# Attention scores of whole jobs: from half-row float32 pairs to two whole-array float32r passes a head

## The chip, the cores and the metric

The kernel runs on one core of one Trainium2 chip. The metric is device time in microseconds of one execution. Three runs of the kernel before were timed; the comparison is between medians.

## The reference, cut to what matters

```
scores = scale * q @ k.T                     # 4 batches, 8 heads, 576 tokens, head size 64
cum    = cumsum(max(s, 0))
scores = where(causal, -1e9, scores + min(-(cum[q] - cum[k]), 0))
attn   = softmax(scores);  x = attn @ v      # x: 2304 tokens x 512
h = x @ w_in;  g = s * relu(h)**2 + b;  y = g @ w_out          # 512 -> 2048 -> 512
out = max(y@w1, y@w2, y@w3) @ w_out2                           # 512 -> 768 -> 512
```

The score of a query and a key is a product over 64 numbers plus a difference of two running sums, the decay. All arithmetic has to be close to float32.

## The kernel before, in words

Matrix products of the two MLPs are made of three float32r passes (`mm3`, lines 245 to 247): each operand is split into hi and lo, and hi·hi, hi·lo and lo·hi are summed in one PSUM bank. float32r is the type in which TensorE takes one pass over the columns.

Attention goes by jobs. A job is a pair of heads of one batch. The four pairs of the first batch are cut into half jobs, A (queries 0 to 319) and B (the rest), 8 in all; the other three batches are 12 whole jobs, W. Queries are cut into chunks of 64, 128, 128, 128 and 128, and the scores of a W job into 6 units of 64, 192, 320, 448, 288 and 288 key columns, 1600 in all (`UNITS`). For each unit `qk` issues four products: for each head a float32 product of q and k over 64 rows (line 468; head 0 on rows 0 to 63, head 1 on rows 64 to 127), and then for each head a float32r product over the same 64 rows (line 470), which adds the decay: `oh` picks the row of the head out of `dd`, the table of decay differences. VectorE adds the causal mask and takes the smallest (`least`, 482), ScalarE takes the exponential (`expo`, 488), TensorE turns the result (`turn_p`, 529), ScalarE or VectorE copies it to SBUF (`copy_p`, by `copy`, 234 or 238), and `av` (548) multiplies by v. The result x is split into hi and lo (GpSimd makes lo, `minus`, 241) for the first MLP.

Products of the first MLP fill TensorE between the steps of attention; the second MLP follows. Beside attention, VectorE, ScalarE and GpSimd also turn the MLP weights from float64 into hi and lo (`weight_steps`, 274 to 289). The first 16 pieces (`wa_in`, `wa_out`) are needed while the half jobs run, and W jobs use their staging memory, so the turned scores of the first W job wait for the last of them. Further pieces (`wb`, `wbs`) are converted beside the W jobs and saved to memory.

The order on every engine is fixed when the program is built. `Plan.order` is a list scheduler: each step has a cost, a due time and needs, and each engine's queue is written in the order that the plan finds. `PORT` and `has_port` make it keep GpSimd's steps and VectorE's conversion steps apart in its own reckoning. On the chip each engine works its queue in order and waits on semaphores. All loads and stores are issued by SP, in order. Score banks, turned scores, transposed reciprocals and their copies share a ring of four PSUM banks (`sm`).

Of the kernel before, what the change touches and what calls it, by code (L numbers as in the profile page):

```python
# [8 lines left out]
F32 = mybir.dt.float32  # L9
# [9 lines left out]
P = 128  # L19
# [13 lines left out]
K_LOAD = -14.0  # L33
V_LOAD = 2.0
# [158 lines left out]
def fused_kernel(ctx, tc, q, k, v, s, w_in, w_out, ms, mb, w1, w2, w3, w_fin, out,  # L193
# [224 lines left out]
    qt, kt, ohs, mns, ps_, pts, rts, rbs, pr, px_, xs_ = ({} for _ in range(11))  # L418
# [44 lines left out]
    def qk(job, u):  # L463
# [120 lines left out]
    def in_us(fixed, each):  # L584
# [8 lines left out]
                 "ws": 2, "wg": 3, "wx": 1, "wb": 3, "p": 3, "ph": 4, "wst": ST2, "wsa": 2, "xs": XS_BUFS, "y0": 2, "y": 2, "g2": 2, "yt": 2, "yh": 2, "u": 2, "o": 2})  # L593
# [30 lines left out]
    add(("pp",), "Pool", 1.2, 4.0, [("pre", "Pool")], rest_p, att=True)  # L624
    jobs = [Job(n, n % NP, "AB"[n // NP]) if n < 2 * NP else Job(n, n - NP, "W") for n in range((B + 1) * NP)]
    t0 = 0.0
    for job in jobs:
# [4 lines left out]
        for u, w in zip(units, widths):  # L632
            at[u] = t
            t += period * w / sum(widths)
# [8 lines left out]
        tp = t0 + TURN  # L643
        for key, when, m in (("q", Q_LOAD, job.q1 - job.q0), ("k", K_LOAD, job.keys)):
            add((key, n), "SP", (1, m), t0 + when, [("qk", n - 2, u) for u in range(6)], load_qk, job, key, **a)
        add(("v", n), "SP", (2, job.keys), t0 + V_LOAD, [("av", n - 2, g) for g in (jobs[n - 2].groups if n > 1 else ())], load_v, job, **a)
        add(("oh", n), "Pool", 0.3, tp, [("qk", n - 2, u) for u in range(6)], one_hot, job, **a)

        for x, u in enumerate(units):
            i, k0, k1, c0, c1 = UNITS[u]  # L650
            same = [("turn_p", n - 1, z, j) for z in range(6) if UNITS[z][0] == i for j in range(2)]
            order = [("after", ("qk", n, units[x - 1]))] if x else [("after", ("qk", n - 1, jobs[n - 1].units[-1]))] if n else []
            ready = [("oh", n), ("q", n), ("k", n)]
            add(("qk", n, u), "PE", 5 * (k1 - k0) / 2400 + 0.25, at[u], ready + [("dd", i) if i > 2 else ("pre", "DVE")] + [("after", z) for z in same] + order, qk, job, u,
                take=[("sm", [("least", n, u, j)]) for j in range(2)], **a)
# [14 lines left out]
        for x, u in enumerate(units):  # L670
            i, k0, k1, c0, c1 = UNITS[u]
            for j in range(2):
                t = at[u] + D_T + 0.2 * j
                before = (n, units[x], 0) if j else (n, units[x - 1], 1) if x else (n - 1, jobs[n - 1].units[-1], 1) if n else None
# [4 lines left out]
                if x == 0:  # L679
# [3 lines left out]
                    over += [("dd", NC - 1)]  # L683
# [426 lines left out]
```

## Time and profile before

| | |
|---|---|
| median of 3 runs | 947.61 us (947.55 to 948.44) |
| span of the profiled execution, first to last instruction | 945.5 us |
| the profiled execution's own time | not listed apart from its span; the median run is 2.1 us above the span |
| TensorE | 925.6 us busy, 98% |
| VectorE, ScalarE, GpSimd | 503.0, 422.2 and 162.2 us busy |

A span is counted from the first to the last instruction. A busy time is the union of the times in which an engine's instructions ran. TensorE's instructions overlap: a product is listed from its start to the modelled end of its drain, so what one costs is read from the distance between the starts of two.

### The profile page before, as it was taken

How to read it: one execution, taken by the hardware profiler on the slowest of the kernel's cores; microseconds unless marked ns; L12 is line 12 of the kernel's file. 1: busy time of each engine (PE TensorE's matmuls, PEld its weight loads, DVE VectorE, ACT ScalarE, POOL GpSimd, SP SyncE). 2: the span in 40 equal slices, each digit the busy share in tenths (PEclk: the TensorE clock that was granted, in tenths of full speed). 3: DMA queues.
4: the chain of work that ended last, by engine and by line, in shares of the span. 5: the costliest groups of instructions: out<-in, count | busy, mean ns of one | idle time of the engine just before them, and what ended most of it. 6: DMA issues, size and time to landing. Idle time of an engine off the chain costs nothing.

```text
span 945.5 us, 16334 instructions
## 1 busy us (share of the span) xinstructions
PE 925.6 (98%) x6016; PEld 848.6 (90%) x6016; DVE 503.0 (53%) x1322; ACT 422.2 (45%) x1126; POOL 162.2 (17%) x255
## 2 busy tenths in 40 slices
PE   7999899999999999999999999999999999999997
PEld 5677677778898799999999999999999999999997
DVE  6999788787833422224686687578621223121221
ACT  5987578888645643333353344344221212121111
POOL 3232122310412043222232133120000000000000
PEclk7999999999999999999999999999999999999999
DMA  7545464465522101912334324334120202010000
GB/s 231 172 122 163 155 197 152 135 192 163 159 80 71 35 16 54 371 55 84 102 121 152 118 85 134 117 117 134 51 68 1 67 1 67 1 51 1 23 12 34
DMA packets 68240, 96.00 MB, mean 102 GB/s; under 512 B 6592, under 2 KB 47296, under 8 KB 68160
## 3 DMA queue, kind: packets, MB, share of 16 engines
q1 hardware_dynamic: 68064, 94.81, 31.4%
q8 instruction: 47, 0.77, 0.3%
q14 instruction: 33, 0.27, 0.1%
q10 hardware_dynamic: 96, 0.15, 0.0%
HBM read 67.67 MB, written 27.26 MB: 100 GB/s over the span
## 4 chain that ended last, share of the span: by engine, by line
PE 90%; DMA 4%; ACT 2%; DVE 2%; SPq 1%; POOL 1%; issue 0%; DVEq 0%; ACTq 0%; POOLq 0%
PE mm L245 24%; PE mm L247 24%; PE mm L246 24%; PE ps L468 6%; PE pt L529 6%; PE px L548 5%; PE ps L470 1%; PE pr L519 1%; DMA xs<-x_d 1%; DMA wb_in<-wb_d 1%; DMA wg<-in_moe_w_in_dram 1%; DMA stage<-in_moe_w_out_dram 1%; ACT pp L488 0%; POOL ga L241 0%; DMA wbs<-in_moe_w_in_dram 0%
## 5 line engine op out<-in xcount | busy, mean ns | idle before, releaser
L245 PE MATMUL mm<-yh,wt 128*128 128x384 f32 x432 | 146.2, 339 | 0.0
L246 PE MATMUL mm<-yl,wt 128*128 128x384 f32 x432 | 146.2, 338 | 0.0
L247 PE MATMUL mm<-yh,wt 128*128 128x384 f32 x432 | 146.2, 338 | 0.0
L1017 DVE TENSOR_TENSOR u<-mm,u 128x384 f32<-128x384 f32 x72 | 40.1, 557 | 185.1 <-PE mm L247 184.9
L881 ACT ACTIVATE g<-g 128x384 f32<-128x384 f32 (+2 forms) x112 | 53.6, 479 | 155.2 <-DVE g L877 155.0
L488 ACT ACTIVATE pp<-pp,mn 64x64 f32<-64x64 f32 (+4 forms) x160 | 88.3, 556 | 12.8 <-DVE mn L482 12.8
L877 DVE TENSOR_SCALAR g<-mm 128x384 f32<-128x384 f32 (+2 forms) x112 | 55.5, 497 | 55.4 <-PE mm L247 49.0
L245 PE MATMUL mm<-ga,wa_out 128*128 128x320 f32 (+2 forms) x256 | 81.8, 320 | 1.5 <-ACT wa_out L234 1.5
L245 PEld LDWEIGHTS mm<-yh,wt 128*128 128x128 f32 x432 | 81.1, 188 | 1.3
L246 PEld LDWEIGHTS mm<-yl,wt 128*128 128x128 f32 x432 | 81.1, 188 | 1.3
L247 PEld LDWEIGHTS mm<-yh,wt 128*128 128x128 f32 x432 | 81.1, 188 | 0.0
L234 ACT ACTIVATE pt<-pt 128x256 f32<-128x256 f32 (+3 forms) x182 | 71.5, 434 | 20.7 <-PE pt L529 17.2
L245 PE MATMUL mm<-xhi,wa_in 128*128 128x320 f32 (+1 forms) x256 | 80.0, 312 | 0.0
L247 PE MATMUL mm<-ga,wa_out 128*128 128x320 f32 (+2 forms) x256 | 75.9, 297 | 3.5 <-DVE wa_out L289 3.5
L1021 ACT ACTIVATE hh<-u 128x384 fp32r<-128x384 f32 x36 | 18.9, 524 | 134.5 <-DVE u L1017 134.5
L529 PE MATMUL pt<-ident,pp 128*128 128x128 f32 x480 | 76.5, 283 | 2.3 <-ACT pt L234 1.0
L468 PE MATMUL ps<-k,q 64*128 64x288 f32 (+4 forms) x384 | 73.0, 449 | 3.8 <-DVE mn L482 3.5
L246 PE MATMUL mm<-ga,wa_out 128*128 128x320 f32 (+2 forms) x256 | 75.9, 297 | 0.5 <-POOL ga L241 0.5
L241 POOL TENSOR_TENSOR gbl<-g,gbh 128x384 fp32r<-128x384 f32 x48 | 51.1, 1064 | 145.0 <-ACT gbh L234 132.4
L247 PE MATMUL mm<-xhi,wa_in 128*128 128x320 f32 (+1 forms) x256 | 75.8, 296 | 0.0
L246 PE MATMUL mm<-xlo,wa_in 128*128 128x320 f32 (+1 forms) x256 | 75.7, 296 | 0.0
L482 DVE CUSTOM_DVE_ANT_0 pp<-late_keys,ps 64x64 f32<-64x64 f32 (+4 forms) x160 | 61.8, 421 | 21.0 <-PE ps L470 20.3
(158 smaller groups left out, 2143.2 us busy)
## 6 DMA issues: line engine op xcount, KB each, us to landing
wst<-in_moe_w_dram SPq DMA_DIRECT2D x24, 384.0 KB, 3.9
wb_d<-wbs SPq DMA_DIRECT2D x21, 256.0 KB, 2.6
k<-in_k_dram SPq DMA_DIRECT2D x16, 288.0 KB, 3.5
xs<-x_d SPq DMA_DIRECT2D x24, 192.0 KB, 3.0
y<-y_d SPq DMA_DIRECT2D x24, 192.0 KB, 3.3
y_d<-y SPq DMA_DIRECT2D x24, 192.0 KB, 2.5
yt<-y_d SPq DMA_DIRECT2D x24, 192.0 KB, 2.5
out_dram<-o SPq DMA_DIRECT2D x18, 256.0 KB, 2.0
```

What stands on the lines that cost most here:

```text
L234: nc.scalar.activation(dst, src, AF.Copy, scale=1.0 if scale is None else scale)
L241: ENGINES[on].tensor_tensor(dst, a, b, op=ALU.subtract)
L245: nc.tensor.matmul(ps, lhs[0], rhs[0], start=first, stop=False)
L246: nc.tensor.matmul(ps, lhs[0], rhs[1], start=False, stop=False)
L247: nc.tensor.matmul(ps, lhs[1], rhs[0], start=False, stop=last)
L468: nc.tensor.matmul(ps[:, :k1 - k0], qt[job.n][r, QS[i]:QS[i] + P], kt[job.n][r, k0:k1], start=True, stop=False)
L482: nc.vector.tensor_tensor_reduce(out=pp[j][i][:n, k0:k1], in0=late_keys[:n, a:a + k1 - k0], in1=ps_.pop((job.n, u, j))[:n, :k1 - k0], scal ...
L488: nc.scalar.activation(p[:n, :w], p[:n, :w], AF.Exp, bias=mns[job.n, j][:n, i:i + 1], scale=-1.0, accum_out=sums[job.n % 2][:n, j, i:i + 1])
L529: nc.tensor.transpose(pt[:, c - c0, :], pp[j][i][:, c * P:(c + 1) * P], ident)
L548: nc.tensor.matmul(px_[job.n][hf][j * D:(j + 1) * D, a0 - h0:h1 - h0], vn[job.n % 2][:, c, j, :], columns(job, pr["p", job.n, j], c, c + 1 ...
L877: nc.vector.tensor_scalar(st["g", f], st["u", f][:, :n], 0.0, None, op0=ALU.max)
L881: nc.scalar.activation(st["g", f], st["g", f], AF.Square)
```

## The change

A W job's scores are computed per head, by two float32r products over all 128 rows. A tile `set` holds four rows of tables for one head. QA is hi of q on rows 0 to 63 and lo of q on rows 64 to 127; KA is hi of k on both halves: their product is hi·hi plus lo·hi. KB has lo of k on rows 64 to 127, QB hi of q there: hi·lo. Rows 0 to 3 of KB and QB hold the running sum in hi and lo and ones, so that the decay comes out of the second product; the other rows of that half are zero, cleared once. So `oh` and the 64-row products remain for half jobs alone.

Making a set takes new steps for each of the 24 heads: a load of q and k, written twice so that both halves of the partitions hold them (`load_both`), one rounding on ScalarE over 128 x 1152 (`round_set`), one subtraction on GpSimd over 64 x 1152 (`rest_set`), one copy over 64 x 576 on GpSimd or ScalarE (`again_set`), and one small load of the decay rows (`decay_set`). Once, at the start, the running sums are split and saved to memory (`decays`, `save_d`) and the sets are cleared. Half jobs load each operand in two loads of 64 partitions in place of one of 128. Units of a W job go through head 0 and then head 1. The host lays q and k out accordingly, and the scratch memory for dynamic DMAs is set to 1024.

```diff
-    qt, kt, ohs, mns, ps_, pts, rts, rbs, pr, px_, xs_ = ({} for _ in range(11))
+    raw, hs_, ohs, mns, ps_, pts, rts, rbs, pr, px_, xs_ = ({} for _ in range(11))
+    QA, KA, KB, QB = range(4)
+    def decays(x, on=None):
+        c = cum[:NH]
+        if x == 0:
+            nc.scalar.activation(dm[:, 0], c, AF.Copy, scale=1.0 / scale)
+        elif x == 1:
+            nc.vector.scalar_tensor_tensor(dm[:, 1], c, 1.0 / scale, dmf[:, 0], op0=ALU.mult, op1=ALU.subtract)
...
+    def save_d():
+        for z in range(2):
+            nc.sync.dma_start(dm_d[:, z, 2 * z:2 * z + 2], dmf[:, 2 * z:2 * z + 2])
+            nc.sync.dma_start(dm_d[:, 1 - z, 2 * z:2 * z + 2], ones[:NH].unsqueeze(1).to_broadcast([NH, 2, S]))
...
     def load_qk(job, key):
 
-        to, src, a, b = (qt, q, job.q0, job.q1) if key == "q" else (kt, k, 0, job.keys)
-        to[job.n] = atp.tile([P, S], F32, name=key, tag=f"{key}{job.n % 2}")
-        nc.sync.dma_start(to[job.n][:, a:b], src[job.p, :, a:b])
+        z, src, a, b = (0, q, job.q0, job.q1) if key == "q" else (1, k, 0, job.keys)
+        if key == "q":
+            raw[job.n] = atp.tile([P, 2, S], F32, name="raw", tag=tag("raw"))
+        for j in range(2):
+            nc.sync.dma_start(raw[job.n][j * D:(j + 1) * D, z, a:b], src[job.p, j, :D, a:b])
+
+    def load_both(job, j):
+
+        t = raw[job.n, j] = atp.tile([P, 2, S], F32, name="raw", tag=tag("raw"))
+        for z, src in ((0, q), (1, k)):
+            nc.sync.dma_start(t[:, z], src[job.p, j])
+
+    def round_set(job, j):
+        hs_[job.n, j] = sets(plan.slot("hs")[1])
+        nc.scalar.activation(hs_[job.n, j][:, :2], raw[job.n, j], AF.Copy)
+
+    def again_set(job, j, on):
+        copy(hs_[job.n, j][D:, QB], raw[job.n, j][D:, 0], on)
+
+    def rest_set(job, j):
+        t = hs_[job.n, j]
+        minus(t[D:, QA:KB + 1:KB], raw[job.n, j][D:], t[D:, :2].bitcast(F32), "Pool")
+
+    def decay_set(job, j):
+        nc.sync.dma_start(hs_[job.n, j][0:4, KB:].bitcast(F32), dm_d[2 * job.p + j].rearrange("t r n -> r t n"))
...
         for r, ps in both:
-            nc.tensor.matmul(ps[:, :k1 - k0], qt[job.n][r, QS[i]:QS[i] + P], kt[job.n][r, k0:k1], start=True, stop=False)
+            nc.tensor.matmul(ps[:, :k1 - k0], raw[job.n][r, 0, QS[i]:QS[i] + P], raw[job.n][r, 1, k0:k1], start=True, stop=False)
...
+    def qk_set(job, u, j):
+        i, k0, k1 = UNITS[u][:3]
+        ps, t = bank("ps"), hs_[job.n, j]
+        for x, (a, b) in enumerate(((QA, KA), (QB, KB))):
+            nc.tensor.matmul(ps[:, :k1 - k0], t[:, a, QS[i]:QS[i] + P], t[:, b, k0:k1], start=x == 0, stop=x == 1)
+        ps_[job.n, u, j] = ps
...
+            for j in range(2):
+                th = t0 + j * period / 2
+                add(("q", n, j), "SP", (2, 2 * S), th + Q_LOAD, [], load_both, job, j, take=[("raw", [("rest", n, j), ("again", n, j)])], **a)
+                add(("round", n, j), "ACT", act(2 * S), th + SET_AT, [("q", n, j)] + [("set", z) for z in range(2)], round_set, job, j, take=[("hs", [("qk", n, u, j) for u in units])], **a)
+                add(("decay", n, j), "SP", (2, 16), th + SET_AT + 1, [("round", n, j), ("save_d",)], decay_set, job, j, **a)
+                add(("rest", n, j), "Pool", pool_(2 * S), th + SET_AT + 1, [("round", n, j)], rest_set, job, j, **a)
+                add(("again", n, j), {"Pool": pool_norm(S), "ACT": act(S)}, 0, th + SET_AT + 1.5, [("round", n, j)], again_set, job, j, **a)
...
-    nc = _bacc.Bacc("TRN2", target_bir_lowering=False, num_devices=1)
+    nc = _bacc.Bacc("TRN2", target_bir_lowering=False, num_devices=1, dynamic_dma_scratch_size=1024)
```

TensorE's queue beside a W job in the middle of attention, before: one visit of two units (448 and 288 columns), two `mm3` groups of the first MLP's second product (`mm<-ga,wa_out`), and the next unit. `ps` is a score bank, `k,q` and `dd,oh` are the operands of lines 468 and 470, and x2 stands for the two heads.

```order
L468 MATMUL ps<-k,q 128x448 x2
L470 MATMUL ps<-dd,oh 128x448 x2
L468 MATMUL ps<-k,q 128x288 x2
L470 MATMUL ps<-dd,oh 128x288 x2
L245 MATMUL mm<-ga,wa_out 128x258
L246 MATMUL mm<-ga,wa_out 128x258
L247 MATMUL mm<-ga,wa_out 128x258
L245 MATMUL mm<-ga,wa_out 128x258
L246 MATMUL mm<-ga,wa_out 128x258
L247 MATMUL mm<-ga,wa_out 128x258
L468 MATMUL ps<-k,q 128x288 x2
L470 MATMUL ps<-dd,oh 128x288 x2
```

The same stretch of the changed kernel; here x2 stands for the two passes of one head's unit, and the third line of `qk_set` is line 531.

```order
L531 MATMUL ps<-set 128x64 x2
L531 MATMUL ps<-set 128x192 x2
L531 MATMUL ps<-set 128x320 x2
L246 MATMUL mm<-ga,wa_out 128x258
L247 MATMUL mm<-ga,wa_out 128x258
L248 MATMUL mm<-ga,wa_out 128x258
L531 MATMUL ps<-set 128x448 x2
L531 MATMUL ps<-set 128x288 x4
L246 MATMUL mm<-ga,wa_out 128x258
L247 MATMUL mm<-ga,wa_out 128x258
L248 MATMUL mm<-ga,wa_out 128x258
```

One head's six units now follow each other with one or two groups of the MLP between. Counted over the whole queue, from the first product with v of the second W job to that of the seventh (five jobs), 55 such groups stood before and 84 stand now; up to the last W job's it is 294 in both.

GpSimd's queue in the same part of attention, before: lo parts of x (`xlo`) and of the MLP's activations (`ga`), the one-hot tables and the reciprocals (`rr`).

```order
L241 TENSOR_TENSOR xlo<-x_0_1873,xhi 128x320
L241 TENSOR_TENSOR xlo<-x_1_1902,xhi 128x256
L458 CAST oh<-rows 128x128
L241 TENSOR_TENSOR ga<-g,ga 128x256
L241 TENSOR_TENSOR ga<-one 128x2
L502 CAST rr<-rs 128x10
L503 TENSOR_TENSOR rr<-rs,rr 128x10
L241 TENSOR_TENSOR ga<-g,ga 128x256
```

And now, with the subtraction and the copy of the sets between them:

```order
L242 TENSOR_TENSOR set<-raw,set 64x2x576
L239 CAST set<-raw 64x576
L242 TENSOR_TENSOR ga<-g,ga 128x256
L242 TENSOR_TENSOR ga<-one 128x2
L242 TENSOR_TENSOR xlo<-x_0_1953,xhi 128x320
L242 TENSOR_TENSOR xlo<-x_1_1977,xhi 128x256
L242 TENSOR_TENSOR ga<-g,ga 128x256
L242 TENSOR_TENSOR ga<-one 128x2
L242 TENSOR_TENSOR set<-raw,set 64x2x576
```

In all GpSimd gains 24 subtractions and 19 copies, ScalarE 24 roundings and 5 copies, and 12 one-hot tables are gone. Of the conversion steps it did 7 and now does 5, all among the first 16 pieces (before, 2 of them).

SP's queue at the start, before: the tables s, then q and k of the first two half jobs, then weights (`wg`) and v (`vn`).

```order
L328 DMA s_110<-in_s_dram 32x576 x2
L428 DMA q<-in_q_dram 128x320
L428 DMA k<-in_k_dram 128x320
L428 DMA q<-in_q_dram 128x320
L428 DMA k<-in_k_dram 128x320
L270 DMA wg<-in_moe_w_in_dram 128x512
L434 DMA vn_115<-in_v_dram 128x2x128
L436 DMA vn_115<-in_v_dram 64x128
```

And now:

```order
L329 DMA s_110<-in_s_dram 32x576 x2
L461 DMA raw<-in_q_dram 64x320 x4
L271 DMA wg<-in_moe_w_in_dram 128x512
L487 DMA vn_115<-in_v_dram 128x2x128
L489 DMA vn_115<-in_v_dram 64x128
L461 DMA raw<-in_k_dram 64x320 x4
L271 DMA wg<-in_moe_w_in_dram 128x512
```

The first half job's k stood second behind s; now four loads of q, one of weights and two of v stand ahead of it.

## Rows read from the trace of the kernel before

**Rows 1.** The page: busy us of each engine, share of the span, instructions.

```profile
PE 925.6 (98%) x6016; PEld 848.6 (90%) x6016; DVE 503.0 (53%) x1322; ACT 422.2 (45%) x1126; POOL 162.2 (17%) x255
```

**Rows 2.** Windows: length, PE, PEld, DVE, ACT, POOL busy, clock, DMA share, GB/s.

```profile
93.00:103.00 10.00, 4.79 (x28) 3.99 (x28) 9.71 (x23) 4.21 (x12) 1.01 (x1) 1.00 0.51 167
120.00:240.00 120.00, 120.00 (x979) 96.00 (x978) 94.63 (x362) 97.37 (x318) 26.46 (x55) 1.00 0.55 169
131.60:215.20 83.60, 83.60 (x694) 65.32 (x694) 66.61 (x253) 69.02 (x230) 19.92 (x42) 1.00 0.54 165
```

**Rows 3.** Windows of the score banks `ps` alone: PE, PEld and DVE busy.

```profile
120.00:340.00 220.00, 51.72 (x384) 31.26 (x384) 51.25 (x128) 1.00 0.41 127
```

**Rows 4.** Timeline of TensorE through one W job: start, busy, line, output and operands.

```profile
189.29 0.28 PE L247 MATMUL mm<-ga,wa_out 128*128 128x258 f32 x1
189.51 1.02 PE L468 MATMUL ps<-k,q 64*128 64x448 f32 x4
...
191.28 0.39 PE L245 MATMUL mm<-ga,wa_out 128*128 128x258 f32 x1
191.50 0.28 PE L246 MATMUL mm<-ga,wa_out 128*128 128x258 f32 x1
191.62 0.28 PE L247 MATMUL mm<-ga,wa_out 128*128 128x258 f32 x1
...
191.98 0.28 PE L247 MATMUL mm<-ga,wa_out 128*128 128x258 f32 x1
...
193.01 1.09 PE L529 MATMUL pt<-ident,pp 128*128 128x128 f32 x8
...
194.06 0.29 PE L246 MATMUL mm<-ga,wa_out 128*128 128x258 f32 x1
...
194.54 0.28 PE L247 MATMUL mm<-ga,wa_out 128*128 128x258 f32 x1
...
195.92 0.28 PE L246 MATMUL mm<-ga,wa_out 128*128 128x258 f32 x1
...
196.59 0.81 PE L468 MATMUL ps<-k,q 64*128 64x320 f32 x4
...
197.47 0.77 PE L529 MATMUL pt<-ident,pp 128*128 128x128 f32 x5
```

**Rows 5.** Timeline of TensorE: starts of float32r products of 320 and 512 columns.

```profile
84.26 0.31 PE L245 MATMUL mm<-ga,wa_out 128*128 128x320 f32 x1
84.41 0.31 PE L246 MATMUL mm<-ga,wa_out 128*128 128x320 f32 x1
...
937.00 0.39 PE L246 MATMUL mm<-wfin,hh 128*128 128x512 f32 x1
937.23 0.39 PE L247 MATMUL mm<-wfin,hl 128*128 128x512 f32 x1
```

**Rows 6.** Groups by shape, ScalarE and GpSimd: count, busy us, mean ns.

```profile
L234 ACT ACTIVATE ga<-g 128x256 fp32r<-128x256 f32 x32 | 13.3, 416 | 0.8
L234 ACT ACTIVATE wa_out<-stage 128x512 fp32r<-128x512 f32 x7 | 4.4, 625 | 0.1
L241 POOL TENSOR_TENSOR ga<-g,ga 128x256 fp32r<-128x256 f32 x32 | 23.7, 742 | 60.9 <-ACT ga L234 60.1 <-PE pt L529 0.7
L241 POOL TENSOR_TENSOR wg<-wg,wa_in 128x512 f32<-128x512 f32 x1 | 1.3, 1323 | 0.5 <-ACT pp L488 0.5
```

**Rows 7.** Timeline of VectorE and GpSimd: one conversion beside a GpSimd step.

```profile
176.29 0.88 DVE L277 TENSOR_SCALAR wbs<-wbs 128x256 int32<-128x256 int32 x1
177.09 0.28 DVE L277 TENSOR_SCALAR wb<-wb 128x256 int32<-128x256 int32 x1
176.28 0.74 POOL L241 TENSOR_TENSOR ga<-g,ga 128x256 fp32r<-128x256 f32 x1 [0.51 <-ACT ga L234]
```

**Rows 8.** Timeline of SP's queue at the start, and DMA issues.

```profile
2.10 0.43 SPq L428 DMA_DIRECT2D k<-in_k_dram  x1
k<-in_k_dram SPq DMA_DIRECT2D x4, 160.0 KB, 4.5
```

More of the change, by code (lines that the diff above doesn't have):

```diff
@@ L33 @@
 K_LOAD = -14.0
+SET_AT = -10.0
 V_LOAD = 2.0
@@ L624, in fused_kernel @@
     add(("pp",), "Pool", 1.2, 4.0, [("pre", "Pool")], rest_p, att=True)
+    for x, e in enumerate(("ACT", "DVE", "DVE", "DVE")):
+        add(("dm", x), e, act(S) if e == "ACT" else dve(S), 8.0 + x, [("pre", "DVE")] + [("dm", y) for y in range(x)], decays, x, att=True)
+    add(("save_d",), "SP", (4, 16), 8.0, [("dm", x) for x in range(4)], save_d, att=True)
+    for z in range(2):
+        add(("set", z), "Pool", 0.9, 20.0, [("save_d",)], clear_set, z, att=True)
     jobs = [Job(n, n % NP, "AB"[n // NP]) if n < 2 * NP else Job(n, n - NP, "W") for n in range((B + 1) * NP)]
     t0 = 0.0
+    qk_key = lambda n, u, j: ("qk", n, u) if n < 2 * NP else ("qk", n, u, j)
     for job in jobs:
@@ L632, in fused_kernel @@
         for u, w in zip(units, widths):
[L633 removed]
+            for j in range(2):
+                at[u, j] = t0 + j * period / 2 + (t - t0) / 2 if n >= 2 * NP else t
             t += period * w / sum(widths)
@@ L649, in fused_kernel @@
+        last_qk = [qk_key(n - 1, jobs[n - 1].units[-1], 1)] if n else []
         for x, u in enumerate(units):
             i, k0, k1, c0, c1 = UNITS[u]
[L651 to L655, printed above, removed]
@@ L656, in fused_kernel @@
-            for j in range(2):
-                add(("least", n, u, j), "DVE", dve(k1 - k0) + 0.08, at[u] + LEAST, [("qk", n, u)] + same + ([("least", n, units[x - 1], j)] if k0 else []), least, job, u, j, **a)
+            if pairs:
+                same = [("turn_p", n - 1, z, j) for z in range(6) if UNITS[z][0] == i for j in range(2)]
+                order = [("after", ("qk", n, units[x - 1]))] if x else [("after", z) for z in last_qk]
+                ready = [("oh", n), ("q", n), ("k", n)]
+                add(("qk", n, u), "PE", 5 * (k1 - k0) / 2400 + 0.25, at[u, 0], ready + [("dd", i) if i > 2 else ("pre", "DVE")] + [("after", z) for z in same] + order, qk, job, u,
+                    take=[("sm", [("least", n, u, j)]) for j in range(2)], **a)
@@ new lines, in fused_kernel @@
+            for j in range(2):
+                same = [("turn_p", n - 1, z, j) for z in range(6) if UNITS[z][0] == i]
+                if not pairs:
+                    order = [("qk", n, units[x - 1], j)] if x else [("qk", n, units[-1], 0)] if j else last_qk
+                    add(("qk", n, u, j), "PE", 2 * max(0.112, mm_cost(k1 - k0)), at[u, j], [("rest", n, j), ("again", n, j), ("decay", n, j)] + [("after", z) for z in same + order], qk_set, job, u, j,
+                        take=[("sm", [("least", n, u, j)])], **a)
+                add(("least", n, u, j), "DVE", dve(k1 - k0) + 0.08, at[u, j] + LEAST, [qk_key(n, u, j)] + same + ([("least", n, units[x - 1], j)] if k0 else []), least, job, u, j, **a)
@@ L668, in fused_kernel @@
             add(("copy_rb", n, hf), {"ACT": act_ps(HN[hf]), "DVE": dve_ps(HN[hf])}, 0, end + R_AT + 1, [("spread_r", n, hf)] + [("x_copy", n - z, hf) for z in range(1, NP + 2)], copy_rb, job, hf, **a)
[L670 to L674, printed above, removed]
+        turns = [(u, j) for j in range(2) for u in units] if n >= 2 * NP else [(u, j) for u in units for j in range(2)]
+        for z, (u, j) in enumerate(turns):
+                x = units.index(u)
+                i, k0, k1, c0, c1 = UNITS[u]
+                t = at[u, j] + D_T + (0.2 * j if n < 2 * NP else 0)
+                before = (n, *turns[z - 1]) if z else (n - 1, jobs[n - 1].units[-1], 1) if n else None
                 order = [("after", ("turn_p", *before))] if before else []
```

38 lines of the change are left out of this document (29 added, 9 removed).

## The prediction

> **What bounds the kernel now.** I read the page first: TensorE is busy for 925.6 us, 98% of the span [rows 1]. Then the windows [rows 2]. From 120 to 240 us, where most of the 12 W jobs lie, TensorE is busy for all of 120.00 us, while VectorE has 94.63, ScalarE 97.37 and GpSimd 26.46: whatever TensorE issues there is paid in full, the products of the first MLP fill every gap that attention leaves, and a microsecond taken out of TensorE's work comes off the end as long as nobody makes it wait. The one stretch with real waiting is 93 to 103 us, where TensorE has 4.79 of 10 us and VectorE 9.71: there the last weight pieces are converted, and W jobs can't turn scores into their memory before. So two questions decide: how much TensorE work goes, and whether another engine begins to hold TensorE up.
>
> **What a W job's scores cost now.** The timeline of one W job [rows 4] has all six units in four visits between other work. Products of 258 columns start 0.12 us apart (191.50 and 191.62). The first visit (448 and 288 columns): from the last product ahead of it, 189.29, to the second behind it, 191.50, are 2.21 us; two products of 0.12 belong to the MLP, so the visit costs 1.97. I go to the second one behind because the first is held up (it starts at 191.28, and its successor 0.22 later, not 0.12); ahead, too, the score starts 0.22 after 189.29. So each visit loses about 0.09 on entering and 0.10 before a product of the MLP. The second (288): 193.01 - 191.98 - 0.12 = 0.91. The third (64 and 192): 195.92 - 194.54 - 0.24 = 1.14. The fourth (320): 197.47 - 196.59 = 0.88, and 0.09 for entering, 0.97. Together 4.99 us. Is this job like the others? The score banks keep TensorE busy for 51.72 us from 120 to 340, in 384 instructions [rows 3]; a job has 36, so these are 10.67 jobs of 4.85. The job above, counted that same way (from a visit's first start to the end of its last product), has about 4.7, so the mean one costs some 3% more, 5.15.
>
> **What they cost after.** Per unit and head two float32r products over all rows, 24 a job, neighbours of products of the same kind. Starts stand 0.12 apart at 258 columns, 0.15 at 320 and 0.23 at 512 [rows 4, 5]; between them I put 288 at 0.135 and 448 at 0.20. For 64 and 192 columns no such product is in the trace. The upper bound is that of 258 columns, 0.12; the lower follows the columns alone, some 0.42 ns each ((0.23 - 0.15) / 192), which gives 0.04 and 0.09. I take 0.12 by the nearest row, the turns of scores: eight of them, of only 128 columns each, and one product take from 193.01 to 194.06 [rows 4], so a turn costs (1.05 - 0.12) / 8 = 0.116, as much as a product of twice its columns. One pass over the six units is then 0.12 + 0.12 + 0.15 + 0.20 + 0.135 + 0.135 = 0.86 us, and four passes (two a head) 3.44; by the lower bound 3.0. Whether entering still costs 0.19 in all I take from the turns too: they work on all 128 rows, and their 0.116 has the change to and from the MLP's products in it. So I charge none here.
>
> **The saving.** For the job shown 4.99 - 3.44 = 1.55, times 12 jobs 18.6 us; for the mean one 1.71, 20.5 us. I take 19.5. With short products at their lower bound it would be 24.7. Half jobs keep their products, from another tile: nothing.
>
> A rule that speaks against this much: FP8 and Floating Point Precision in the Trainium skill (TensorE Precision Notes) has true FP32 make four passes through the array. By that alone a pair of heads takes 4 + 1 passes over its columns side by side on half rows now and 2 x 2 after: 1600 columns less a job, an estimated 0.67 us at 0.42 ns, and 8 us in all; the time would be that of rival B. The rows don't fit it: 5 passes over 1600 columns would be 3.4 us, and the job shown costs 4.99. I keep the rows.
>
> **What is added beside it.** Per head: one rounding on ScalarE of 1152 elements. 256 take 0.416 and 512 take 0.625 us [rows 6], 0.82 ns an element, so 1.15 us. One GpSimd subtraction of 1152: 256 take 0.742 and 512 take 1.323 [rows 6], 2.27 ns an element, so 2.8 us. One copy of 576, on GpSimd 19 times of 24: not in the trace in this form; between 0.65 (as ScalarE) and 1.4 (as the subtraction), I take 1.1, since GpSimd is the slower in every row. Does each have room? The window 131.6 to 215.2 [rows 2] runs from the second W job's product with v to the seventh's: five jobs of 16.7 us. By the order listing these jobs have 29 more MLP groups than before, 5.8 a job; three products of 0.12 to 0.15 make some 0.38 us a group. TensorE's work is then 16.7 - 1.6 + 2.2 = 17.3 us a job.
> ScalarE: 69.02 / 5 = 13.8, two roundings 2.3, the MLP groups' share (two steps of 0.42 to every four products' groups of the first half, so 16 steps to 64 groups) 0.6, the odd copy 0.2: 16.9 us, 97% of TensorE's.
> VectorE: 13.3 and 0.5 for the same groups: 13.8.
> GpSimd: 4.0, two subtractions 5.6, copies 1.7, groups 0.5, the one-hot away: 11.5, from a quarter of the time to two thirds.
> So nobody is over TensorE on paper, but ScalarE is within 3% and the order is fixed: a late exponential holds up a turn, and behind that turn stand the MLP's products. Lower bound nothing; upper bound some 1 us a job (ScalarE at 18.2 against 17.3, if its new steps took half as long again) over the 8 jobs in which it is this full, up to 240 us: 8 us. I take 4, nearer to the lower because the same queue at 13.8 of 16.7 showed no waiting at all.
>
> GpSimd's longer steps also hold up VectorE: a conversion of 256 elements took 0.88 us next to a GpSimd subtraction of 0.74 that began with it, and 0.28 right after [rows 7]; it ran on to about the other's end. Five or six such steps fall on a job. If they met GpSimd by chance, at two thirds of the time, each for half of what it meets (0.9 us on average), that is 3.4 us a job, and VectorE has 17.2 of 17.3. I count it within the 4.
>
> The doubled loads are 24 x 0.59 MB in place of half of that, 7 MB more over some 220 us or 32 GB/s, beside 169 GB/s at a DMA share of 0.55 [rows 2]: hidden, 0.1 of share. If a set came late, its first unit would wait and the MLP behind it too.
>
> **The start.** The first half job's k was issued at 2.10 us and landed about 4.5 later [rows 8]; now seven more issues of 0.43 to 0.6 stand ahead, so it lands some 3.4 us later, and with it the first scores. VectorE can convert weights meanwhile, and it is VectorE that the stretch to 103 us hangs on. Its work up to the last weight stays about level: three conversion steps of 0.7 fewer, five small steps for the decay tables. Two roundings and two subtractions of the first W job fall in that stretch too. I take 1 us late, between 2 early (if fewer conversions count in full) and 4 late (if k's delay goes through).
>
> **The sum.** -19.5 + 4 + 1 = -14.5 us. From the profiled span of 945.5 that is 931; the median run lies 2.1 above that span, so 933.1.
>
> **Rivals.**
> A. As above: TensorE's saving with a few waits, 933.1; its own range from -20.5 - 2 = 925 (921 with the short products at their lower bound) to -18.6 + 8 + 4 = 941.
> B. The losses of 0.09 and 0.10 at a visit aren't those of half rows and stay with the new products. By the order a job's scores then stand in about five visits: 5 x 0.19 = 0.95 us a job, 11.4 in all, and of 19.5 us 8.1 are left; less the same 5, 944.5. For it: scores still stand between turns and the MLP. Against it: the turns' 0.116.
> C. GpSimd holds up VectorE, and the kernel is slower. The place is the conversions beside W jobs; the price is what VectorE has above 17.3 us a job, over the 7 jobs from 120 to 240. It decides at 18.5 / 7 = 2.6 us a job over, which is 6.1 us of waiting, each of the conversion steps meeting a subtraction of 2.8 us and waiting more than a third of it. At half (1.4 us each, 8 us a job) VectorE has 21.8, 4.5 over, 31 us in all: 960. For it: rows 7, and two subtractions a job. Against it: from 120 to 240 GpSimd was busy for 22% of the time and VectorE never late for TensorE, and the planner keeps the two apart in its reckoning. GPSIMD Engine Reference in the Trainium skill (Key points) has GpSimd share its SBUF interfaces with VectorE and names contention with two-port modes and two-input steps; rows 7 agree.
> D. The saving is there and taken back in full: ScalarE's 16.9 grows to 19.3, 2 us a job over TensorE in 8 jobs, and the start loses 4: 20 against 19.5, within 0.2%, 946 to 949. Its roundings would have to take twice 1.15 for that.
>
> **How the numbers follow.** A 0.74, B 0.10, C 0.09, D 0.07. 0.2% of 947.6 is 1.9 us, about what a measurement of this kernel can tell from no change. A and most of B are faster by more: 0.84; D and a part of B within it: 0.07; C slower: 0.09. The range from 923 to 943 holds A but for its far end, and stops short of B, C and D.
>
> **What would show it.** Right: TensorE busy throughout from about 105 us to 340; starts of the `set` products as close as those of the MLP, a pass over six units near 0.86; the end of attention some 15 us earlier, and the stretch behind it unchanged. Wrong: TensorE idle before turns, waiting on ScalarE's exponentials or on VectorE's minima; conversions of 256 elements at 1 us and more; a last weight piece later than 104 us; a set that its first unit waits for.

## The result, and the profile after

The median is 938.43 us in four runs (936.99 to 942.0), against 948.03 us (947.55 to 948.70) for four runs of the kernel before beside them: a ratio of 0.9904, 95% interval 0.9882 to 0.9927. So the kernel is faster by 9.6 us; the forecast was 933.1.

The page of the changed kernel: busy us of each engine, share of the span, instructions. Its span is 935.2 us.

```profile
PE 904.8 (97%) x5872; PEld 850.8 (91%) x5872; DVE 518.1 (55%) x1327; ACT 448.0 (48%) x1158; POOL 243.9 (26%) x286
```

Beside [rows 1]: TensorE is busy 20.8 us less, and as the span shrank by 10.3, its idle time grew by 10.5, from 19.9 to 30.4 us. The last product with v starts at 339.0 us, against 350.0 before: attention ends 11 us earlier, where some 15 were forecast, and the stretch behind it is as long as it was. The windows show where (length, PE, PEld, DVE, ACT, POOL busy, clock, DMA share, GB/s):

```profile
20.00:40.00 20.00, 12.81 (x77) 8.61 (x78) 15.32 (x47) 12.21 (x43) 6.90 (x7) 0.66 0.49 147
...
93.00:103.00 10.00, 10.00 (x77) 8.63 (x76) 9.82 (x20) 5.97 (x17) 6.71 (x7) 1.00 0.55 168
103.00:120.00 17.00, 14.32 (x103) 13.27 (x103) 16.29 (x52) 13.62 (x41) 7.81 (x7) 1.00 0.40 126
120.00:240.00 120.00, 118.71 (x972) 106.78 (x969) 94.64 (x344) 115.31 (x343) 73.89 (x74) 1.00 0.64 196
240.00:340.00 100.00, 96.61 (x779) 88.68 (x779) 62.92 (x196) 72.53 (x207) 42.90 (x48) 1.00 0.38 120
```

From 120 to 240 us ScalarE went from 97.37 [rows 2] to 115.31 us, GpSimd from 26.46 to 73.89, VectorE stayed at 94.6, and TensorE, never idle there before, is idle for 1.3 us; from 240 to 340 for 3.4. Summed over the windows up to 120 us, it is idle for 19.9 us, 5.8 more than before; from 120 to 340 for 4.7, 4.5 more. What it waits for up to 120 us, and then from 120 to 340 (total, times, longest):

```profile
PE pt L589 <- ACT pt L235: 11.8, 1, 11.8
PE mm L248 <- DVE wa_out L290: 2.7, 1, 2.7
...
PE mm L246 <- DVE ya L1016: 1.3, 1, 1.3
PE pt L589 <- ACT pt L235: 0.8, 1, 0.8
```

The 11.8 us end at 27 us. ScalarE's timeline ahead of that shows why a copy of turned scores is so late: it stands in ScalarE's queue behind conversions that wait for weights.

```profile
22.40 0.69 ACT L275 ACTIVATE stage<-wst 128x512 f32<-128x512 f32 x1 [2.69 <-DMA wst<-in_moe_w_in_dram]
24.65 0.70 ACT L275 ACTIVATE wg<-wg 128x512 f32<-128x512 f32 x1 [1.56 <-DMA wg<-in_moe_w_in_dram]
25.26 0.61 ACT L235 ACTIVATE wa_in<-wg 128x512 fp32r<-128x512 f32 x1
25.78 1.13 ACT L235 ACTIVATE wa_in<-stage 128x512 fp32r<-128x512 f32 x2
26.82 0.85 ACT L235 ACTIVATE pt<-pt 128x64 f32<-128x64 f32 x4
```

The 2.7 us end at 106.6 us, when the last but one of the steps that write `wa_out` is done; the last one is done 0.6 us later, and the copies of the first W job's turned scores start right behind it, at 107.2. Of `wa_out`, VectorE's last steps (count, min/median/max ns, first and last start) are in the kernel before, and then in the changed one:

```profile
L289 DVE TENSOR_TENSOR wa_out<-stage x6: 681/688/1221, 68.7 to 102.3; 128x512 fp32r<-128x512 f32 x6
```

```profile
L290 DVE TENSOR_TENSOR wa_out<-stage x6: 661/684/821, 62.2 to 106.5; 128x512 fp32r<-128x512 f32 x6
```

The last piece comes 4.2 us later. Below it is dated by the start of this last step, 102.3 and 106.5.

The products themselves, from TensorE's timeline (start, busy, line, operands, count):

```profile
194.14 0.46 PE L531 MATMUL ps<-set 128*128 128x320 f32 x2
194.44 0.27 PE L589 MATMUL pt<-ident,pp 128*128 128x128 f32 x1
194.47 0.66 PE L531 MATMUL ps<-set 128*128 128x448 f32 x2
194.97 0.28 PE L246 MATMUL mm<-ga,wa_out 128*128 128x258 f32 x1
195.08 0.28 PE L247 MATMUL mm<-ga,wa_out 128*128 128x258 f32 x1
...
195.33 0.43 PE L531 MATMUL ps<-set 128*128 128x288 f32 x2
195.60 0.28 PE L246 MATMUL mm<-ga,wa_out 128*128 128x258 f32 x1
195.72 0.28 PE L247 MATMUL mm<-ga,wa_out 128*128 128x258 f32 x1
```

Two passes of 320 columns take 0.30 us to the next start, two of 288 take 0.27 (195.33 to 195.60), and the MLP's next products follow at their own 0.12, with none of the 0.09 and 0.10 that a visit lost in [rows 4]. A turn of 128 columns and two passes of 448 take 0.53 together (194.44 to 194.97): with the 0.12 of a turn, the two passes come to the 0.40 forecast.

### The profile page after: what moved, and what is told of

Same layout as the page of the kernel before. It is cut to its first block, busy times and chain, and to the rows that moved or that the text cites. A ratio compares the mean times of both kernels' runs of the same rounds, so it can differ in the third digit from the quotient of the medians.

```text
span 935.2 us, 16309 instructions
## 1 busy us (share of the span) xinstructions
PE 904.8 (97%) x5872; PEld 850.8 (91%) x5872; DVE 518.1 (55%) x1327; ACT 448.0 (48%) x1158; POOL 243.9 (26%) x286
## 4 chain that ended last, share of the span: by engine, by line
PE 82%; DMA 6%; DVE 5%; ACT 4%; SPq 2%; issue 1%; POOL 1%; POOLq 0%; ACTq 0%; DVEq 0%
PE mm L246 23%; PE mm L248 23%; PE mm L247 23%; PE pt L589 4%; PE px L608 4%; PE ps L531 3%; PE ps L521 1%; DMA xs<-x_d 1%; DMA stage<-in_moe_w_in_dram 1%; DVE pp L542 1%; DMA raw<-in_k_dram 1%; ACT pt L235 1%; PE pr L579 1%; POOL ga L242 1%; DMA wb_in<-wb_d 1%
## 5 line engine op out<-in xcount | busy, mean ns | idle before, releaser
L589 PE MATMUL pt<-ident,pp 128*128 128x128 f32 x480 | 79.0, 280 | 15.9 <-ACT pt L235 12.5
L548 ACT ACTIVATE pp<-pp,mn 128x192 f32<-128x192 f32 (+4 forms) x160 | 88.8, 559 | 2.7 <-DVE mn L542 2.5
L242 POOL TENSOR_TENSOR set<-raw,set 64x1152 fp32r<-64x1152 f32 x24 | 65.1, 2712 | 61.4 <-ACT set L471 55.9
L246 PE MATMUL mm<-xhi,wa_in 128*128 128x320 f32 (+1 forms) x256 | 79.8, 312 | 1.3 <-DVE ya L1016 1.3
L589 PEld LDWEIGHTS pt<-ident,pp 128*128 128x128 f32 x480 | 56.1, 142 | 24.7 <-ACT pt L235 14.3
L242 POOL TENSOR_TENSOR ga<-g,ga 128x320 fp32r<-128x320 f32 (+1 forms) x64 | 54.0, 845 | 87.4 <-ACT ga L235 85.2
```

The costliest lines, as they stand in the source:

```text
L242: ENGINES[on].tensor_tensor(dst, a, b, op=ALU.subtract)
L246: nc.tensor.matmul(ps, lhs[0], rhs[0], start=first, stop=False)
L548: nc.scalar.activation(p[:n, :w], p[:n, :w], AF.Exp, bias=mns[job.n, j][:n, i:i + 1], scale=-1.0, accum_out=sums[job.n % 2][:n, j, i:i + 1])
L589: nc.tensor.transpose(pt[:, c - c0, :], pp[j][i][:, c * P:(c + 1) * P], ident)
```

## The experiments

All are timed beside the kernel before on the same chip (its medians there: 947.6 to 948.4 us). The changed kernel was not timed again beside them, so a difference of a microsecond or so against its 938.4 us means little; the ratios, each to the kernel before, are the safer numbers.

**e1 and e2: a single load for each operand, then the saves later too.**

```diff
-        for j in range(2):
-            nc.sync.dma_start(raw[job.n][j * D:(j + 1) * D, z, a:b], src[job.p, j, :D, a:b])
+        nc.sync.dma_start(raw[job.n][:, z, a:b], src[job.p, :, :D, a:b])
...
-[] if key == "q" else [("q", n)]
+[] if key == "q" else [("issue", "q", n)]
```

In e2 also `save_d` due at 40 in place of 8, with ones of its own to save, and the clearing of the sets due at 45 in place of 20.

> A half job's q and k come in one load of 128 partitions each, and k is planned behind the issue of q instead of behind its landing; all else as in the changed kernel. Theory S (what is missing against the forecast was lost at the start: SP's queue is filled by the split loads, the weight loads go out late, and the 11.8 us wait of TensorE at 27 us and the last weight piece at 107.2 us follow): the wait at 27 us shrinks by more than half, the last weight piece lands at 104 to 106 us, and the time is 934 to 937 us. Rival M (the missing part was lost beside the W jobs): the start moves, but the time stays at 938, within 1 us.

> As the run before, and the four saves of the decay tables go out behind the weight loads of the start instead of between them. Theory S: nothing new stands ahead of the weights in SP's queue, the last piece is there at about 103 us as in the kernel before, and the time is 932 to 935 us (938.4 less 4 to 6). Rival M: 938, within 1 us.

Measured: 976.06 us (ratio 1.0298, 1.0280 to 1.0315) and 973.51 us (1.0281, 1.0256 to 1.0306), far from both theories. The DMA view of e1 from 4 to 13 us (busy tenths and GB/s, 40 slices), and SP's timeline:

```profile
DMA  9549899862111111111111111111111111111011
GB/s 108 108 118 342 332 373 379 337 240 71 46 46 46 46 46 46 46 51 51 46 46 46 46 46 46 46 46 46 46 46 46 58 42 55 55 55 55 30 57 46
```

```profile
3.56 5.92 SPq L460 DMA_DIRECT2D raw<-in_k_dram  x2
9.52 3.71 SPq L486 DMA_DIRECT2D vn<-in_v_dram  x1
```

From 6 us on a tenth of the DMA engines' time moves 46 GB/s, and SP stands in the issues of k and then of v for 5.9 and 3.7 us. TensorE waits 7.8 us for k in one piece, and 14.1 us for k in all up to 120 us. These two say nothing on the start; they raise a question of their own, which e5 answers.

**e3: the old scores behind the new start.** W jobs take the branch of the half jobs (`pairs` true for all jobs), so `qk` and not `qk_set`.

> The changed kernel with its start (split loads, decay tables, saves, cleared tiles), but with the half-row float32 scores for W jobs too and so without the steps that fill the sets. Theory S: the start costs 5 to 6 us by itself, so 948.0 + 5.5 = 953 to 954 us, and the last weight piece is at 107 us. Rival M: the start costs about the 1 us of the forecast, 948 to 950 us.

Measured: 949.19 us, ratio 1.0021 (1.0003 to 1.0039), 1 to 2 us over the kernel before by the medians and 0.3 to 3.7 by the interval. Theory S falls: the loads, decay tables and saves of the start cost about what was forecast. The twelve runs spread widely, from 945.4 to 954.1 us, and the profiled one is the shortest of them. In it the wait at 27 us is there all the same (11.0 us), and the last weight piece is not late:

```profile
L290 DVE TENSOR_TENSOR wa_out<-stage x6: 660/680/1228, 61.4 to 102.5; 128x512 fp32r<-128x512 f32 x6
```

So the long wait of TensorE costs little: TensorE, which before idled 5.2 us of the ten ahead of 103 us [rows 2], is now busy for all ten, and reaches the last weight piece as it is ready.

**e4 and e10: sets filled once, and not even that.**

```diff
-        minus(t[D:, QA:KB + 1:KB], raw[job.n, j][D:], t[D:, :2].bitcast(F32), "Pool")
+        if job.n == 2 * NP:
+            minus(t[D:, QA:KB + 1:KB], raw[job.n, j][D:], t[D:, :2].bitcast(F32), "Pool")
```

and so for rounding, copy and decay load; in e10 only the first job's roundings are left of them.

> Leaves out the filling of the sets (rounding, subtraction, copy and decay load) for every W job but the first; the scores of the others use what the sets hold. The q and k loads stay, and so does the order of all other instructions. Theory S: at most the 4.5 us of idle time that TensorE gained from 120 to 400 us come back, 934 to 938 us. Rival M: the filling costs more than TensorE's idle time shows, and 7 us or more come back, 931 us or less. Were the new idle time only due to the new order of the queues, nothing would come back: 938.

> e4, which filled the sets of the first W job alone, without that job's two subtractions, copies and decay loads as well (only its two roundings are left; the clearing of the sets covers all partitions); order unchanged. Theory: the start costs the changed kernel 3 to 4 us because its last weight piece is written at 107.2 us instead of 102.9, and what is late is VectorE, whose conversion steps GpSimd's subtractions of the first W job stretch: without them the piece is written by 105 us, and the time is 933 to 935 us (e4: 936.2). Rival: the planner's order puts that piece later by itself: 107 us again, and 936.

Measured: e4 936.21 us (ratio 0.9876, 0.9859 to 0.9892), e10 933.98 us (0.9865, 0.9842 to 0.9888). In both TensorE is idle for under 2 us from 120 to 340, against 4.7. By the medians filling the sets costs 2.2 to 4.4 us, then, in line with the 4 forecast, and M's 7 are not there. (Against the changed kernel's 0.9882 to 0.9927 the interval of e4 overlaps and that of e10 just touches, so the 2.2 alone would not tell filling from nothing.) The last pieces, e4's and then e10's:

```profile
L290 DVE TENSOR_TENSOR wa_out<-stage x6: 660/682/829, 66.2 to 110.6; 128x512 fp32r<-128x512 f32 x6
```

```profile
L290 DVE TENSOR_TENSOR wa_out<-stage x6: 662/682/1343, 63.1 to 106.3; 128x512 fp32r<-128x512 f32 x6
```

Without any of the subtractions the piece comes at 106.3, as in the changed kernel (106.5): the theory of e10 falls and its rival's mechanism, the order of the queues, stands. That the time, 934.0, lies in the theory's range is luck. e4's piece comes 4 us after e10's in the same order; the granted clock from 20 to 40 us was 0.50 in e4 and 0.67 in e10, and the same steps already lie 3 us apart at 80 us.

What the order does can be read in the traces. The last weight load waits for a buffer that VectorE's step on `wa_out` frees. In e3 (first) and in the changed kernel (second; SPq is SP's queue, and the last line is its wait ahead of that load, from 89.6 us on):

```profile
82.32 0.43 DVE L284 TENSOR_SCALAR stage<-stage 128x512 int32<-128x512 int32 x1
84.17 1.51 POOL L242 TENSOR_TENSOR stage<-stage,wa_out 128x512 f32<-128x512 f32 x1
87.13 0.68 DVE L290 TENSOR_TENSOR wa_out<-stage 128x512 fp32r<-128x512 f32 x1
88.00 0.38 SPq L271 DMA_DIRECT2D stage<-in_moe_w_out_dram  x1
```

```profile
82.51 3.13 POOL L242 TENSOR_TENSOR set<-raw,set 64x1152 fp32r<-64x1152 f32 x1 [0.34 <-POOL ga L242]
89.66 0.42 DVE L284 TENSOR_SCALAR stage<-stage 128x512 int32<-128x512 int32 x1
91.34 0.68 DVE L242 TENSOR_TENSOR stage<-stage,wa_out 128x512 f32<-128x512 f32 x1
95.23 0.82 DVE L290 TENSOR_TENSOR wa_out<-stage 128x512 fp32r<-128x512 f32 x1
96.08 0.34 SPq L271 DMA_DIRECT2D stage<-in_moe_w_out_dram  x1
SPq L271 <- DVE wa_out L290: 6.4, 1, 6.4
```

Up to 82 us the two are within 1 us of each other. Then VectorE's steps on this piece come 7 us later, and the subtraction among them, which is GpSimd's in e3, is VectorE's, while GpSimd has the first set. So the load goes out 8 us later, and half of that is made up by the end. In e10 it goes out at 95.52, though the set's subtraction is not there: the place in the order is what counts. No run moved this one piece alone.

**e5 and e6: e1 and e2 with plain rows.** Memory holds head 0 twice and then head 1 twice, so rows 64 to 191 are what a half job needs.

```diff
-        nc.sync.dma_start(raw[job.n][:, z, a:b], src[job.p, :, :D, a:b])
+        nc.sync.dma_start(raw[job.n][:, z, a:b], src[job.p].rearrange("j d n -> (j d) n")[D:3 * D, a:b])
```

> As e1 (one load of 128 partitions for each operand of a half job, k planned behind the issue of q), but the source is 128 rows in one row stride (rows 64 to 191 of the four copies that memory holds for a pair) and no longer two groups of 64 rows. Theory F (e1 lost its 28 us because a source of two groups was carried by few of the 16 DMA engines: 0.1 of their share, 45 GB/s from 4 to 12 us): q and k land within 5 us, the SP queue doesn't stand, and the time is 935 to 938 us. Theory O (e1 lost them by its order, k ahead of v and of the second weight load): 965 us or more again.

> As e2 (saves of the decay tables behind the weight loads of the start), with the plain rows of e5. Theory F: 934 to 937 us, up to 3 us of the start come back against the changed kernel, since e3 showed that its start costs only about 1.6 us. Theory O: 965 us or more.

Measured: e5 943.04 us (ratio 0.9926, 0.9900 to 0.9952), e6 944.09 (0.9951, 0.9935 to 0.9967). The order is that of e1 and e2 but for this load form, and 33 and 29 us are gone: theory F holds on the cause, the form of the load. Its number doesn't: neither is better than the changed kernel. e5's six runs lie in two groups, 937 to 938 and 943 to 945; the profiled one is of the upper, with a clock of 0.50 from 20 to 40 us and the last piece at 110.5. The mean clock of the two short ones was 0.986 and 0.989, of the four long ones 0.981 to 0.983. In e6 TensorE's long wait is gone and the clock from 20 to 40 is 0.99, and the time is no better:

```profile
20.00:40.00 20.00, 17.46 (x128) 11.70 (x126) 18.45 (x61) 16.88 (x59) 6.36 (x11) 0.99 0.56 164
93.00:103.00 10.00, 2.02 (x6) 1.62 (x7) 8.77 (x14) 2.43 (x4) 1.67 (x1) 0.63 0.60 197
```

The last piece comes at 108.5, and TensorE, earlier with everything else, idles 8 us of the ten ahead of 103. (This execution, 940.97 us, is the shortest of six.)

**e7, e8: one filling step doubled.** The rounding, or the subtraction, is issued twice in a row. In e8 the second subtraction puts other numbers into QA, which changes the scores.

> The changed kernel with the rounding of every set done twice on ScalarE (24 more steps of about 1.05 us), the order otherwise the same. If ScalarE, at 115.3 of 120 us from 120 to 240, is what holds TensorE up beside the W jobs, it now has 130 us of work there, and the time rises by 8 to 15 us, to 946 to 953. If its waits hide in slack of the queues, the time rises by less than 3 us.

> The changed kernel with the subtraction of every set done twice on GpSimd (24 more steps of 2.7 us), the order otherwise the same; GpSimd goes from 74 to some 112 of 120 us from 120 to 240. Rival C's mechanism (a long GpSimd step holds up VectorE's conversions, and these TensorE): the time rises by 8 us or more, 946 or later, and conversions of 256 elements take 1.2 us and more. If GpSimd costs nothing as long as it is not full, the time rises by less than 3 us.

Measured: e7 956.24 us (ratio 1.0089, 1.0070 to 1.0108), e8 988.57 us (1.0433, 1.0412 to 1.0454), 18 and 50 us over the changed kernel; the 956 lie beyond the 946 to 953 expected. The windows from 120 to 240, e7's and then e8's:

```profile
120.00:240.00 120.00, 111.14 (x885) 96.21 (x885) 89.20 (x312) 117.95 (x326) 68.11 (x70) 1.00 0.56 173
```

```profile
120.00:240.00 120.00, 99.09 (x745) 87.86 (x745) 100.31 (x274) 91.75 (x268) 87.14 (x69) 0.93 0.50 155
```

ScalarE's 25.3 us more over the whole run (473.3 busy against 448.0) cost 18, GpSimd's 67.0 more (310.9 against 243.9) cost 50, about 0.7 to 0.75 us for each. Neither hides its added work. GpSimd was expected to reach 112 of 120 us and got no further than 87: what waits for it holds it up in turn (set, scores, least value, exponential), which is argued from the order and not tested. TensorE's waits in e8 from 120 to 340 show both ways in which it holds up the rest, its own late results and VectorE's late ones:

```profile
PE pr L568 <- POOL rr L564: 9.2, 6, 2.4
PE pr L580 <- ACT rt L235: 5.7, 1, 5.7
PE ps L532 <- POOL set L242: 4.9, 3, 2.4
PE ps L532 <- DVE mn L543: 4.1, 2, 2.4
```

Conversions of 256 elements on `wbs` (lines 280, 284 and 286) take 0.55, 0.75 and 0.80 us on the mean from 120 to 240, against 0.44, 0.39 and 0.48 in the changed kernel. So rival C's mechanism is seen at twice the dose, but short of the 1.2 us expected, and GpSimd's own late results (14.1 us of TensorE's waits on the lines shown) weigh more than VectorE's.

**e9: rounding on VectorE.**

```diff
-                add(("round", n, j), "ACT", act(2 * S), th + SET_AT,
+                add(("round", n, j), "DVE", dve_fast(2 * S) - 0.06, th + SET_AT,
```

> The changed kernel with the rounding of every set on VectorE instead of ScalarE, in the order that the planner then finds. e7 says that ScalarE holds TensorE up beside the W jobs. If that is all of the new waiting there, ScalarE falls from 115 to about 100 of 120 us from 120 to 240, TensorE's 4.7 us of idle time from 120 to 340 fall below 2, and the time is 934 to 937 us. If VectorE (94.6 of 120 us, and GpSimd stretches its steps) takes ScalarE's place, idle time stays and the time is 938 or more.

Measured: 945.88 us, ratio 0.9993 (0.9974 to 1.0012): no gain clear of noise is left. ScalarE did fall to 103.0 us, VectorE rose to 103.8, and TensorE's idle time from 120 to 340 grew from 4.7 to 8.0. Most roundings take less there than ScalarE's 1146 to 1201 ns, but some take up to 2.2 us (min, median and max below), 1055 ns in the mean from 120 to 240. One of 1.72 us, from 126.03, began beside a GpSimd subtraction that ran to 127.14. The planner also gave ScalarE 16 of the 24 copies, in place of 5. The first wait is now VectorE's:

```profile
L471 DVE CAST set<-raw x24: 699/760/2226, 80.6 to 307.1; 128x1152 fp32r<-128x1152 f32 x24
```

```profile
PE pt L589 <- DVE mn L542: 3.7, 3, 2.1
```

**e11 and e12: due times of the weights moved forward.** In e11 on the base of e5 with the second head's roundings on VectorE, in e12 on the base of e6.

```diff
-W_S1 = 4.607
-W_2 = 29.041
-W_S2 = 2.532
+W_S1 = 4.701
+W_2 = 24.19
+W_S2 = 2.205
```

So in e12, where the decay tables are also due at 20 in place of 8; 4.217, 27.27 and 2.393 in e11.

> The changed kernel with due times of the weight pieces moved forward (27.27 + 2.393 a piece for 29.04 + 2.532, and 4.217 for 4.607), plain rows and k behind the issue of q as in e5, and the second head's rounding on VectorE. Theory W (what the start costs is the time of the last weight piece: 107.2 us in the changed kernel, 111.2 in e5 with 943.0 us, 109.2 in e6 with 944.1): by the order built, the piece comes 1 to 3 us before that of the changed kernel, and ScalarE has 7 us less from 120 to 240: 933 to 937 us. Rival (loads and TensorE's long wait at 27 us set the cost of the start): no gain beyond e5's, 940 us or more.

> As e6 (plain rows, k behind q, decay tables saved behind the weights), with the weight pieces due sooner (24.19 + 2.205 a piece for 29.04 + 2.532; 4.701 for 4.607), and the decay tables due at 20 in place of 8; the roundings stay on ScalarE. In e6 TensorE no longer waited 11 us at 27 us, and yet the last weight piece was written at 109.2 us and the time was 944.1. Theory W (the time of that piece, which the order of the conversion steps sets, is what the start costs): it comes by 104 us and the time is 933 to 937 us, under the changed kernel's 938.4. Rival (what e6 lost, it lost beside the W jobs, where ScalarE and VectorE have no slack for another order): the piece comes sooner, but TensorE's idle time from 120 to 340 us is 5 us or more, and the time stays at 940 or above.

Measured: e11 947.83 us (ratio 1.0006, 0.9989 to 1.0023), e12 938.40 us (0.9887, 0.9866 to 0.9907). In e11 the piece was not sooner (107.3) and TensorE was idle for 11.9 us from 120 to 340, the largest part waiting for VectorE's least values (5.6): it says again what e9 said, and nothing on the start. In e12 the piece comes 3.5 us sooner than in e6, and the median falls by 5.7 us (the two profiled executions lie 3.2 apart):

```profile
L290 DVE TENSOR_TENSOR wa_out<-stage x6: 683/686/1247, 66.8 to 105.0; 128x512 fp32r<-128x512 f32 x6
```

A microsecond of the six may be idle time, which went from 6.9 to 5.9 from 120 to 340. Theory W has the direction, not the 104 us nor the gain over the changed kernel: the two are equal within their intervals. The rival is half right: the idle time stayed above 5 us, but the time went below 940. e12's mean clock was 0.982 to 0.984 in its five runs, for 935.1 to 939.1 us; the changed kernel's one run at 0.983 took 942.0. So a part of what e12 gains may have been lost to the clock, which no run here separates. No version that does all the work is clear of the changed kernel.

## Why the prediction was nearly right

The forecast was 14.5 us and 9.6 came by the medians: the mechanism is there, and a third of the gain is not.

**The saving (19.5) came, 1 to 4 us short.** TensorE's busy time fell by 20.8 us, but a part of that is not scores. At its lower level (a granted clock of 0.50, 1.2 GHz) TensorE was busy for 12.1 us in the kernel before and for 6.5 in the changed one (windows as above, the first two before, the third changed):

```profile
11.50:21.80 10.30, 8.67 (x37) 5.70 (x38) 8.84 (x35) 9.66 (x33) 0.68 (x3) 0.50 0.71 244
103.70:107.10 3.40, 3.40 (x16) 2.08 (x14) 2.10 (x7) 1.46 (x4) 0.90 (x1) 0.50 0.54 185
```

```profile
16.50:33.60 17.10, 6.53 (x33) 4.40 (x33) 13.17 (x33) 8.72 (x24) 5.50 (x5) 0.50 0.56 177
```

A half job's unit of 320 columns, the same products in both, took 1.52 us there (before, 20.12 to 21.64) and 0.88 at 1.00 (changed, 34.22 to 35.10); by that an estimated 2.3 us of the 20.8 (0.42 of 5.6) are the clock's, and 18.5 are left. With the start's loads in both, from e3 (920.4 us busy) to the changed kernel it is 15.6 us, and to e10, with almost nothing filled, 17.5. The spacing of the passes is that of the MLP's, and rival B, by which visits go on losing 0.19, is refuted by the timeline above. By the four passes of true FP32 that the Trainium skill states (TensorE Precision Notes, FP8 and Floating Point Precision) an estimated 8 us would have been saved; the rows do not agree with that sum here.

**The waits beside W jobs (4) were right.** TensorE's idle time from 120 to 340 us grew by 4.5, and leaving the filling out gave 2.2 (e4) and 4.4 us (e10). The loads on the engines were sized well: rounding 1.16 us (forecast 1.15), subtraction 2.70 (2.8), copy on GpSimd 0.70 (1.1), from 120 to 240 us:

```profile
L242 POOL TENSOR_TENSOR set<-raw,set 64x1152 fp32r<-64x1152 f32 x14 | 37.7, 2695 | 25.2 <-ACT set L471 22.1 <-POOL ga L242 1.6 <-DMA raw<-in_q_dram 1.3
L471 ACT ACTIVATE set<-raw 128x1152 fp32r<-128x1152 f32 x14 | 16.3, 1162 | 0.0
L239 POOL CAST set<-raw 64x576 fp32r<-64x576 f32 x10 | 7.0, 700 | 0.1
```

ScalarE at 96% was forecast at 97, and e7 shows that it was the margin of the whole case: another 1.1 us a head would have cost the gain and more. Rival D needed ScalarE's new steps to take twice as long, and they took what was forecast. Rival C needed VectorE's conversions to wait for GpSimd; VectorE's busy time from 120 to 240 us did not grow (94.63 and 94.64 us), and e8, with twice the subtractions, shows what would have come of it.

**The start (1) is the term that was sized worst: the last weight piece was 4.2 us late.** The step reads "Its work up to the last weight stays about level ... I take 1 us late", and the range ended at 4. It looked at the right quantity, the last weight piece, named 104 us as the bound, and then worked out its time from loads and from VectorE's amount of work. The loads are as forecast: they cost 1 to 2 us (e3). VectorE had less to convert, if anything: by the traces GpSimd did one step of the first 16 pieces before, not two, and now does five. What was left out is the order. The steps that fill the first sets and the scores of the first W job change what stands ahead of that piece in the queues, and which engine does which of its steps. With the same loads of the start the piece comes at 102.5 us with the old scores (e3) and at 106.3 with the new, though nothing is subtracted (e10); in both the clock from 20 to 40 us was the same (0.68 and 0.67). The lines under e10 show where: the last weight load goes out 8 us later, behind a buffer that VectorE frees late. Over the profiles with the changed start the piece by and large follows that load: loads at 88.0, 91.4, 93.5, 95.5, 96.1, 97.9, 99.0 and 100.2 us (e3, e9, e12, e10, changed, e7, e6, e4) go with pieces at 102.5, 105.1, 105.0, 106.3, 106.5, 108.2, 108.5 and 110.6; e11, with 92.6 and 107.3, is out of line.

What this cost the kernel can't be told as exactly. TensorE's idle time up to 120 us was 14.1 us before, 16.7 in e3, 21.0 in e10 and 19.9 in the changed kernel, 5.8 more than before; some 2.3 us of that came back, by the estimate above, as TensorE worked less at the lower clock. That leaves about 3.5 us net, between the 1 taken and the 4 that the range allowed. The sum is then -18.5 + 4.5 + 3.5 = -10.5 where -14.5 was forecast; the span shrank by 10.3. This shares out one measured difference, busy and idle, and is no test of the terms. The rest up to the median is the execution: the profiled one took 936.99 us, 1.4 less than the median.

What stays open is whether that piece alone makes up the difference. The 11.8 us of TensorE at 27 us, the largest wait in the trace, are not it alone: e3 has 11.0 of them at 1 to 2 us in all, and e6 is without them and slower. Still in e10, and so not excluded as a part of it, are the doubled loads of the first W jobs in SP's queue and two roundings. The smaller scratch memory for DMAs and other orders of the first W job were not tried. That the runs of one program spread by the clock is on record for each run: in e3 the four shortest (945.4 to 947.9 us) had a mean clock of 0.989 to 0.991 and the four longest (952.0 to 954.1) of 0.979 to 0.981.

## What to carry to other kernels

Price a stretch that ends with a gate (here the last weight piece) by when the gate opens, and look in the new order of the queues at what stands ahead of it: the longest wait in the trace may cost little, and a step that moves back in its queue or to another engine may put the gate off by 4 us. Where one engine sets the time, sum every other engine against the time that will be left: with ScalarE at 96% and GpSimd at 62% from 120 to 240 us the change still paid, and each microsecond more on either cost about 0.7. Moving a step from one nearly full engine to the next was no cure here (e9). And before a fall in busy time is booked as saved work, look at how much of it ran at the lower clock.

## What the chip showed that I had not expected

A load whose 128 rows lay in memory as two groups of 64 ran at 46 GB/s with a tenth of the DMA engines' time, and held up every load behind it: 976.1 us for the kernel in e1, against 943.0 with the same data as 128 rows of one stride (e5). The two loads of 64 rows that the change has show none of that.

In every kernel in which TensorE waits 11 to 12 us up to 26 to 28 us, the granted clock from 20 to 40 us was 0.50 to 0.68 on the mean, so at its lower level (1.2 GHz) for two thirds of the stretch to all of it. Without that wait it was 0.96 (before), 0.78 (e12) and 0.99 (e6); e1 and e2, which wait for loads instead, had 0.50 and 0.59. But the kernel before and e6 had a stretch at 0.50 too, and TensorE worked in it: from 11.5 to 21.8 us in the kernel before, where it had been busy for 0.9 of the 4 us up to 12, and from 16 to 20 us, all of them busy, in e6. In the changed kernel the stretch was 16.5 to 33.6 us, and TensorE was idle for more than half of it. So a stretch at 0.50 near the start came with the wait and without it; with the wait it lay later, and TensorE did less in it.

VectorE's rounding of 128 x 1152 took 760 ns in the median and up to 2226 (e9), and up to 3178 in e11, where ScalarE's took 1146 to 1201 in the changed kernel: VectorE is the faster in most steps and the slower in those that meet a long GpSimd step.
